# Feature groups with the heads innermost, and the constants of Ln as immediates, in a two-layer linear-attention kernel

## The chip, the cores and the metric

The kernel runs on one core of a Trainium2 chip. A core has five engines that this text speaks of: TensorE (PE in the profile; the loading of its weights is PEld), VectorE (DVE), ScalarE (ACT), GpSimd (POOL) and SyncE (SP), which here issues DMAs. They share an on-chip memory of 128 partitions, SBUF. TensorE writes its results to a second memory, PSUM. The metric is the device time of one execution in microseconds (us), as the median of several runs. Beside it stands one profiled execution, with its own time.

## The reference

`x` has 2048 rows of 512 numbers in bf16. Two layers follow each other, each of an attention and an MLP, both behind a layer norm and added to `x`:

```python
x = x + A(layernorm(x))      # attention
x = x + B(layernorm(x))      # MLP; this pair twice, with the same weights

def A(x):
    q, k, v = x @ wqkv                        # 32 heads of 16 each
    pq, pk = q @ w_phi[h], k @ w_phi[h]       # per head, 16 x 16
    phi_q = concat(softmax(pq), softmax(-pq)) # 32 features
    phi_k = concat(softmax(pk), softmax(-pk))
    kv, z = phi_k^T v, sum of phi_k over the rows
    return (phi_q kv / (phi_q z + 1e-6)) @ wo

def B(x):                                     # F = 1376
    return (relu(x @ W_gate) * (x @ W_up)) @ W_down
```

The layer norm divides by `sqrt(variance + 1e-5)`.

## The kernel before, in words

The 2048 rows are 16 tiles `t` of 128 rows, one row to a partition. `X` holds them in SBUF for the whole run.

**The softmax.** A softmax doesn't change when the same number is taken from all 16 inputs, so the kernel subtracts the last of them: 15 differences remain (`DF`), and the 16th Exp is 1. The subtraction is folded into the weights (`wf`, line 422; `Wblk`, line 426, a block-diagonal matrix of `w_phi` made from `wf` and the mask `Mf`; `Wk2` and `Wq2`, lines 481 to 486). TensorE then gives, for one tile, 480 differences of keys (line 596) or queries (line 656). ScalarE raises them twice, with scale 1 and -1 (line 568, `raised`), into a tile `ek` of 8 groups of 128 elements. A group belongs to four heads: 4 x 15 features for the plus sign, 4 x 15 for the minus sign, and 8 numbers that stand for the 16th features.

**The sums.** VectorE sums each run of 15 features, 64 sums for a tile (line 606 for keys, `sk`; line 661 for queries, `sq`). ScalarE takes Ln(1 + sum) and Exp of its negative (lines 615 and 618 for keys, 666 and 668 for queries), which is the reciprocal. For keys that goes into the last 8 of a group, and all 120 features are multiplied by their scale (`halves`, line 554, in two instructions of four groups each, each on GpSimd or VectorE). For queries VectorE makes the ratio of the two signs (line 672), and only the plus half is multiplied by it (line 677, GpSimd or VectorE).

**The rest of the attention.** The keys' features meet `v` in the state (`kvz`, line 629), which is summed over all 16 tiles. Then it is multiplied by a mask `Mg` that keeps each head's own block (`R`, lines 641 and 646). The queries' features are transposed by DMA (`fq`, line 682) and multiplied by `R` (line 693). The quotient (lines 700 to 707), `wo` (line 716) and the addition to `x` with a row sum (line 720) follow. The layer norm ahead of the attention takes statistics on VectorE (lines 510 and 511), Ln(variance + 1e-5) and Exp(-0.5 ...) on ScalarE (lines 518 and 520).

**The MLP** is gate and up (line 793), relu and product (lines 797 to 812), down (line 833) and the addition to `x` (line 840), in blocks of 1, 2 or 4 tiles.

**The order.** Every instruction's place is written out by hand: `ORDER` is the order in which all steps are issued, `SLOTS` says which buffer each takes, and `PLACE` on which of two engines a step runs where it has a choice. So each engine works a fixed list, and waits by semaphores for what its next instruction needs. The costs and due times that stand with each step no longer decide anything. The keys of all 16 tiles of a layer must be done before its state is, and layer 0's keys, queries and first MLP blocks share the first 80 us.

The lines that the change starts from (before):

```python
def features(ek, lo=0, n=NG):
    return ek.t[:, lo:lo + n, 0:2 * GF].rearrange("p g (j f) -> p g j f", f=DF)
...
v = features(ek, lo, n)
e.tensor_tensor(out=v, in0=v, in1=ek.t[:, lo:lo + n, 2 * GF:P].unsqueeze(3).to_broadcast(
    [P, n, 2 * HG, DF]), op=Alu.mult)
```

with `NG` = 8 groups, `HG` = 4 heads in a group, `DF` = 15 features, `GF` = 60.

Of the kernel before, what the change touches and what calls it, by code (L numbers as in the profile page):

```python
# [8 lines left out]
P = 128  # L9
# [4 lines left out]
NB = D // P  # L14
# [110 lines left out]
DVE0 = (85, 170)  # L125
# [3 lines left out]
NOTHING = (0, 0)  # L129
# [151 lines left out]
def kernel(  # L281
    ctx: ExitStack, tc: tile.TileContext, A_x, A_wqkv, A_w_phi, A_wo, B_x, B_W_gate, B_W_up,
    B_W_down, out):
    nc = tc.nc
# [8 lines left out]
    def new(name, shape, dt=BF16):  # L293
        return sb.tile([P] + shape, dt, name=name)
# [14 lines left out]
    wf = new("wf", [NB, DH])  # L309
    wgu, wd = new("wgu", [2, NB, F]), new("wd", [NF, D])  # L310
    ident = new("ident", [P])
    Mf, Mg, Mh = new("Mf", [HB], F32), new("Mg", [HG], F32), new("Mh", [HG], F32)
    Wblk = new("Wblk", [NB, HB * DF])
    R = new("R", [NG, GE])
    xnTA = [new(f"xnTA{c}", [C, NB, P]) for c in range(C)]
    eps, unit = new("eps", [1], F32), new("unit", [1], F32)
    rowsum, ssq = new("rowsum", [2, T], F32), new("ssq", [2, T], F32)
    wasteA, wasteD = new("wasteA", [D]), new("wasteD", [D])
    st = {(l, s): (new(f"bst{s}{l}", [T, 6], F32), new(f"mv{s}{l}", [T, 2], F32),
# [25 lines left out]
    def op(eng, cost, due, emit, deps=(), takes=(), uses=(), name="", **kw):  # L345
        o = Op(eng, cost, due, emit, deps, takes, uses, name, **kw)
        ops.append(o)
        return o
# [71 lines left out]
    c_m = op("DVE", (230, 330), 10, masks, [c_id], name="masks")  # L420
# [2 lines left out]
                                in1=wf[:, :, DF:DH].to_broadcast([P, NB, DF]), op=Alu.subtract)  # L423

    def blocks(e):
        e.tensor_tensor(
            out=Wblk[:].rearrange("p b (j f) -> p b j f", f=DF),
            in0=wf[:, :, 0:DF].unsqueeze(2).to_broadcast([P, NB, HB, DF]),
            in1=Mf[:].unsqueeze(1).unsqueeze(3).to_broadcast([P, NB, HB, DF]), op=Alu.mult)

    c_cen = op("DVE", (200, 290), 20, against_last, [l_wf], name="wcen", port=True)
    c_blk = op("DVE", (640, 740), 20, lambda: blocks(nc.vector), [c_m, c_cen], name="Wblk", port=True,
               alt=("POOL", (1016, 1058), lambda: blocks(nc.gpsimd), 3))
    def state_masks():
        nc.vector.tensor_reduce(out=Mg[:], in_=ident[:, 0:2 * GF].rearrange("p (s h f) -> p h s f", s=2, f=DF),
                                axis=AX.XY, op=Alu.add)
        nc.vector.tensor_reduce(out=Mh[:], in_=ident[:, 2 * GF:P].rearrange("p (s h) -> p h s", s=2), axis=AX.X,
                                op=Alu.add)
        nc.vector.tensor_tensor(out=Mg[:], in0=Mg[:], in1=Mh[:], op=Alu.add)
    c_mg = op("DVE", (400, 490), 15000, state_masks, [c_m], name="Mg")  # L440
    wps = Buf(p_q)

    one = nc.const_aps.tensor(1.0, (P, 512), BF16)
# [69 lines left out]
    def norm_A(l, tiles, dues, afters, by_pe=False):  # L513

        _, mv, rs, ln = st[l, "A"]
        t0, n = tiles[0], len(tiles)
        seen = [stats(l, "A", t, due, after) for t, due, after in zip(tiles, dues, afters)]
        a = op("ACT", ACT1, dues[-1], lambda: nc.scalar.activation(
            out=ln[:, t0:t0 + n], in_=mv[:, t0:t0 + n, 1], func=AF.Ln, scale=1.0, bias=eps[:]), seen + [c_eps], name="ln")
        a = op("ACT", ACT0, dues[-1], lambda: nc.scalar.activation(  # L520
            out=rs[:, t0:t0 + n], in_=ln[:, t0:t0 + n], func=AF.Exp, scale=-0.5), [a], name="rstd")
        made, i = [], 0
        while i < n:
            k = 1 if by_pe or i + 1 == n else 2
            xn, scaled = Buf(p_xn), []
            for j in range(k):
                t = tiles[i + j]

                def on_pool(t=t, j=j, xn=xn):
                    nc.gpsimd.tensor_scalar(out=nm[:, t:t + 1], in0=mv[:, t, 0:1], scalar1=-1.0, scalar2=0.0,  # L530
                                            op0=Alu.mult, op1=Alu.add)
                    nc.gpsimd.tensor_scalar(out=xn.t[:, j], in0=x_of(t), scalar1=nm[:, t:t + 1],
                                            scalar2=rs[:, t:t + 1], op0=Alu.add, op1=Alu.mult)
                scaled.append(op("DVE", SCALE, dues[i + j], lambda t=t, j=j, xn=xn: nc.vector.tensor_scalar(
                    out=xn.t[:, j], in0=x_of(t), scalar1=mv[:, t, 0:1], scalar2=rs[:, t:t + 1],
                    op0=Alu.subtract, op1=Alu.mult), [a], [] if j else [xn], [xn] if j else [], name="xnA", port=2,
                    alt=("POOL", (930, 975), on_pool, 3) if l == 0 else None))
            c, r = tiles[i] // C, tiles[i] % C
            made += [turn(xn, lambda c=c, r=r, k=k: xnTA[c][:, r:r + k], k, dues[i], scaled, [], [], "xnTA",
                          by_pe)] * k  # L540
            i += k
        return made


    def features(ek, lo=0, n=NG):
        return ek.t[:, lo:lo + n, 0:2 * GF].rearrange("p g (j f) -> p g j f", f=DF)

    def halves(name, ek, engs, due, after, uses):
        parts = []
        n = NG // len(engs)  # L550

        def phi(e, lo):
            v = features(ek, lo, n)
            e.tensor_tensor(out=v, in0=v, in1=ek.t[:, lo:lo + n, 2 * GF:P].unsqueeze(3).to_broadcast(  # L554
                [P, n, 2 * HG, DF]), op=Alu.mult)
        for k, e in enumerate(engs):
            ways = {"DVE": ("DVE", dve(480), lambda k=k: phi(nc.vector, k * n), 1),
                    "POOL": ("POOL", (956, 998), lambda k=k: phi(nc.gpsimd, k * n), 3)}
            _, cost, f, _ = ways[e]
            parts.append(op(e, cost, due, f, after, [], uses, name=name,  # L560
                            port=ways[e][3], alt=ways["POOL" if e == "DVE" else "DVE"]))
        return parts

    def raised(ek, ps, s, side):
        assert side == "K" or ek.slot in ONES and ek.slot not in spoilt
        if side == "K":
            spoilt.add(ek.slot)
        nc.scalar.activation(out=ek.t[:, :, s * GF:(s + 1) * GF], in_=ps.t[:, 0:FW].rearrange(  # L568
            "p (g e) -> p g e", e=GF), func=AF.Exp, scale=1.0 - 2.0 * s)

    class Keys:
        def __init__(self, l, before):
# [8 lines left out]
        def begin(self, sk, row, t, due, due_v, due_z, xT, phi_eng, v_eng="ACT"):  # L581
            c, i = t // C, t % C
            kp, vp = Buf(p_a), Buf(p_b)
            ek, vx = Buf(p_ek), Buf(p_v)
# [10 lines left out]
            else:  # L595
# [8 lines left out]
            v = evac(v_eng, due_v, lambda: vx.t[:, :, 0:GQ], lambda: vp.t[:].rearrange("p (b e) -> p b e", e=GQ),  # L604
                     [v] + ones, [vx], [vp], "vext")
            a = op("DVE", SUM16, due, lambda: nc.vector.tensor_reduce(  # L606
                out=sk.t[:, row, :].rearrange("p (g j) -> p g j", g=NG), in_=features(ek), axis=AX.X, op=Alu.add),
                e, [] if row else [sk], [ek, sk] if row else [ek], name="sk")
            self.sk.append(a)
            self.ks.append(k)  # L610
# [2 lines left out]
        def finish(self, begun):  # L613
            (done, v, sk, ek, *rest), due = begun[0], begun[0][5]
            a = op("ACT", RLN[0], due, lambda: nc.scalar.activation(  # L615
                out=sk.t[:, 0, :], in_=sk.t[:, 0, :], func=AF.Ln, scale=1.0, bias=unit[:]), [done, c_eps], (), [sk],
                name="lnk")
            a = op("ACT", REXP[0], due, lambda: nc.scalar.activation(  # L618
                out=ek.t[:, :, 2 * GF:P], in_=sk.t[:, 0, :].rearrange("p (g j) -> p g j", g=NG), func=AF.Exp,
                scale=-1.0), [a], (), [sk, ek], name="rk")  # L620
            self.scale(a, v, ek, *rest)
# [31 lines left out]
    def query(l, t, due, xT, behind, key):  # L653
        c, i = t // C, t % C
        qp, ek, sq, fq = Buf(p_a), Buf(p_eq), Buf(p_sq), Buf(p_fq)
# [3 lines left out]
        e = [op("ACT", act(FW), due, lambda s=s: raised(ek, qp, s, "Q"), [q], (), [qp, ek], name="Eq")  # L659
             for s in range(2)]  # L660
        a = op("DVE", SUM16, due, lambda: nc.vector.tensor_reduce(  # L661
            out=sq.t[:].rearrange("p (g j) -> p g j", g=NG), in_=features(ek), axis=AX.X, op=Alu.add),
            e, [sq], [ek], name="sq", follow=behind)
        pos, neg = (lambda: sq.t[:].rearrange("p (g s h) -> p g s h", s=2, h=HG)[:, :, 0, :],
                    lambda: sq.t[:].rearrange("p (g s h) -> p g s h", s=2, h=HG)[:, :, 1, :])
        a = op("ACT", RLN[0], due, lambda: nc.scalar.activation(
            out=pos(), in_=pos(), func=AF.Ln, scale=1.0, bias=unit[:]), [a, c_eps], (), [sq], name="lnq")
        a = op("ACT", REXP[0], due, lambda: nc.scalar.activation(
            out=pos(), in_=pos(), func=AF.Exp, scale=-1.0), [a], (), [sq], name="rq")

# [2 lines left out]
                                   op1=Alu.mult)  # L673

        def scale(e):
            v = ek.t[:, :, 0:GF].rearrange("p g (h f) -> p g h f", f=DF)
            e.tensor_tensor(out=v, in0=v, in1=ek.t[:, :, 2 * GF:2 * GF + HG].unsqueeze(3).to_broadcast(  # L677
                [P, NG, HG, DF]), op=Alu.mult)
# [167 lines left out]
    p = PAR  # L846
# [3 lines left out]
    for t in range(T):  # L850
# [8 lines left out]
        sk = begun[0][2] if begun else Buf(p_sk)  # L859
# [92 lines left out]
```

## Time and profile before

| | |
|---|---|
| median of 3 runs | 371.65 us (371.59 to 1351.57) |
| profiled execution | 371.77 us |
| its span, first to last instruction | 370.0 us |
| PE busy | 361.4 us (98%) |
| DVE busy | 272.0 us (74%) |
| ACT busy | 203.4 us (55%) |
| POOL busy | 86.6 us (23%) |
| granted TensorE clock | 1.00 throughout |

One of the three runs took 1351.57 us; the other two agree within 0.06 us. A group's row in the profile reads: line, engine, operation, output and input tiles, shapes, count, then busy time in us and the mean of one in ns, then the idle time ahead of it and what ended that. A row of a table by stage reads: stretch of the span, its length, then busy time and number of instructions of each engine. Busy time of PE is modelled, since matrix multiplications are pipelined: 98% busy is not PE at its peak.

### The profile page before, as it was taken

To read this page: it belongs to the slowest core of one execution; us is meant where nothing else is said; L and a number is where in the kernel's file an instruction comes from. 1 tells how busy PE (TensorE), PEld (TensorE's weight loads), DVE (VectorE), ACT (ScalarE), POOL (GpSimd) and SP (SyncE) were. 2 spreads that over 40 slices of the span, in tenths; PEclk is the share of its full clock that TensorE was granted. 3 is DMA by queue.
4 is the path that set the end of the run, shared out by engine and by line. 5 is a ranking of instruction groups with operands and counts; after the bars stand their busy time and mean duration, and the time that the engine had idled before them with its cause. 6 is when DMAs were issued, how large, how long until landed. Compare 5 with 4: busy or idle time off the path is not lost.

```text
span 370.0 us, 7444 instructions
## 1 busy us (share of the span) xinstructions
PE 361.4 (98%) x2803; PEld 217.0 (59%) x2845; DVE 272.0 (74%) x604; ACT 203.4 (55%) x549; POOL 86.6 (23%) x111
## 2 busy tenths in 40 slices
PE   8999999999999999999999999999999999999996
PEld 5454557776555454555666655686755454467484
DVE  6999999988798966848979498898976373233253
ACT  5999999662544860587274455874434226403130
POOL 4589754510030116004213173120000000000000
PEclk9999999999999999999999999999999999999999
DMA  8997776796653501113411210498752102010213
GB/s 239 195 225 161 235 123 128 128 151 126 96 101 58 99 16 30 37 22 64 85 36 31 57 32 0 69 134 121 137 99 45 28 0 44 0 44 0 81 54 98
DMA packets 93925, 31.73 MB, mean 86 GB/s; under 512 B 85345, under 2 KB 92865, under 8 KB 93889
## 3 DMA queue, kind: packets, MB, share of 16 engines
q1 hardware_dynamic: 93088, 30.98, 42.4%
q8 instruction: 22, 0.36, 0.4%
q10 hardware_dynamic: 800, 0.28, 0.3%
q14 instruction: 15, 0.11, 0.1%
HBM read 8.44 MB, written 2.10 MB: 28 GB/s over the span
## 4 chain that ended last, share of the span: by engine, by line
PE 84%; ACT 9%; DVE 2%; issue 1%; DMA 1%; POOL 1%; SPq 0%; DVEq 0%; ACTq 0%
PE b L793 38%; PE b L833 20%; PE b L716 7%; ACT ek L568 4%; PE b L601 4%; PE b L596 4%; PE b L656 4%; PE b L769 3%; PE q L693 2%; PE q L629 1%; ACT vext L453 1%; DMA X<-in_A_x_dram 1%; DVE sq L661 1%; ACT sk L615 1%; PE b L500 1%
## 5 line engine op out<-in xcount | busy, mean ns | idle before, releaser
L793 PE MATMUL b<-xnTB,wgu 128*128 128x128 bf16 (+2 forms) x1200 | 152.5, 279 | 0.1
L793 PEld LDWEIGHTS <-wgu 128*128 128x128 bf16 x1200 | 97.4, 98 | 47.2 <-issue 0.3
L797 ACT ACTIVATE gu<-b 128x512 bf16<-128x512 f32 (+1 forms) x83 | 47.6, 581 | 89.9 <-PE b L793 83.0
L833 PE MATMUL b<-wd,hT 128*128 128x512 bf16 (+3 forms) x340 | 83.2, 372 | 1.3
L568 ACT ACTIVATE ek<-b 128x480 bf16<-128x480 f32 x128 | 69.9, 597 | 16.1 <-PE b L596 8.6
L554 POOL TENSOR_TENSOR ek<-ek 128x480 bf16<-128x480 bf16 x48 | 49.5, 1055 | 79.2 <-ACT ek L618 74.6
L833 PEld LDWEIGHTS <-hT 128*128 128x128 bf16 (+1 forms) x363 | 34.3, 98 | 34.0 <-DVE hT L810 0.3
L810 DVE TENSOR_TENSOR hT<-gu,b 128x512 bf16<-128x512 bf16 (+1 forms) x44 | 28.6, 657 | 30.3 <-ACT gu L797 13.7
L677 POOL TENSOR_TENSOR ek<-ek 128x480 bf16<-128x480 bf16 x26 | 26.4, 1023 | 73.7 <-DVE ek L672 55.9
L661 DVE TENSOR_REDUCE sq<-ek 128x64 f32<-128x960 bf16 x32 | 36.4, 1144 | 4.1 <-ACT ek L568 4.1
L606 DVE TENSOR_REDUCE sk<-ek 128x64 f32<-128x960 bf16 x32 | 36.0, 1138 | 2.5 <-ACT ek L568 2.5
L801 DVE TENSOR_TENSOR hT<-gu 128x512 bf16<-128x512 bf16 (+1 forms) x39 | 17.2, 442 | 22.6 <-ACT gu L812 22.4
L840 DVE SCALAR_TENSOR_TENSOR X<-b,rsB,X 128x512 bf16<-128x512 f32 (+2 forms) x33 | 23.7, 729 | 12.9 <-PE b L833 12.7
L716 PE MATMUL b<-wo,oT 128*128 128x512 bf16 x117 | 30.8, 379 | 1.1 <-ACT oT L453 0.4
L601 PE MATMUL b<-wv,xnTA 128*128 128x512 bf16 x120 | 30.9, 379 | 0.6 <-ACT vext L453 0.2
L656 PE MATMUL b<-Wq,xnTA 128*128 128x480 bf16 x128 | 30.5, 365 | 0.1
L596 PE MATMUL b<-Wk,xnTA 128*128 128x480 bf16 x124 | 29.5, 366 | 0.0
L720 DVE SCALAR_TENSOR_TENSOR X<-b,X 128x512 bf16<-128x512 f32 x32 | 21.7, 684 | 6.0 <-PE b L716 5.8
L812 ACT CAST gu<-b 128x512 bf16<-128x512 f32 (+1 forms) x39 | 21.9, 573 | 6.8 <-PE b L793 6.6
L510 DVE BATCH_NORM_STATS2 bstA<-X 128x6 f32<-128x512 bf16 x32 | 21.4, 683 | 2.0 <-DMA X<-in_A_x_dram 1.7
L707 DVE TENSOR_TENSOR o<-q,rd 128x512 bf16<-128x512 f32 x32 | 21.9, 686 | 1.3 <-ACT rd L704 1.0
L601 PEld LDWEIGHTS <-xnTA 128*128 128x128 bf16 x128 | 12.0, 98 | 12.7 <-issue 0.3
(84 smaller groups left out, 346.4 us busy)
## 6 DMA issues: line engine op xcount, KB each, us to landing
out_dram<-X SPq DMA_DIRECT2D x15, 128.0 KB, 1.9
X<-in_A_x_dram SPq DMA_DIRECT2D x6, 256.0 KB, 4.8
wgu<-in_B_W_gate_dram SPq DMA_DIRECT2D x4, 344.0 KB, 3.7
wgu<-in_B_W_up_dram SPq DMA_DIRECT2D x4, 344.0 KB, 4.9
wd<-in_B_W_down_dram SPq DMA_DIRECT2D x5, 256.0 KB, 3.7
hT<-in_A_wqkv_dram SPq DMA_DIRECT2D x3, 256.0 KB, 4.4
X<-in_A_x_dram SPq DMA_DIRECT2D x4, 128.0 KB, 3.4
wv<-in_A_wqkv_dram SPq DMA_DIRECT2D x2, 256.0 KB, 4.8
```

What stands on the lines that cost most here:

```text
L554: e.tensor_tensor(out=v, in0=v, in1=ek.t[:, lo:lo + n, 2 * GF:P].unsqueeze(3).to_broadcast([P, n, 2 * HG, DF]), op=Alu.mult)
L568: nc.scalar.activation(out=ek.t[:, :, s * GF:(s + 1) * GF], in_=ps.t[:, 0:FW].rearrange("p (g e) -> p g e", e=GF), func=AF.Exp, scale=1.0 ...
L596: k = op("PE", mm(4, FW), due, lambda: [nc.tensor.matmul(kp.t[:, 0:FW], lhsT=xnTA[c][:, i, b, :], rhs=Wk2[:, b, :], start=(b == 0), stop=( ...
L601: v = op("PE", mm(4, 512), due_v, lambda: [nc.tensor.matmul(vp.t[:], lhsT=xnTA[c][:, i, b, :], rhs=wv[:, b, :], start=(b == 0), stop=(b == ...
L606: a = op("DVE", SUM16, due, lambda: nc.vector.tensor_reduce(out=sk.t[:, row, :].rearrange("p (g j) -> p g j", g=NG), in_=features(ek), axi ...
L656: q = op("PE", mm(4, FW), due, lambda: [nc.tensor.matmul(qp.t[:, 0:FW], lhsT=xnTA[c][:, i, b, :], rhs=Wq2[:, b, :], start=(b == 0), stop=( ...
L661: a = op("DVE", SUM16, due, lambda: nc.vector.tensor_reduce(out=sq.t[:].rearrange("p (g j) -> p g j", g=NG), in_=features(ek), axis=AX.X, ...
L716: a = op("PE", mm(4, 512), due + 3, lambda j=j, yp=yp: [nc.tensor.matmul(yp.t[:], lhsT=oT.t[:, j, b, :], rhs=wo[:, b, :], start=(b == 0), ...
L793: nc.tensor.matmul(ps.t[:, q * W:(q + 1) * W].rearrange("p (i t) -> p i t", t=P), lhsT=wgu[:, s, b, g * P:(g + 1) * P], rhs=xT.t[:, 0:n, b ...
L797: nc.scalar.activation(out=gu.t[:, 0, 0:cols], in_=gp.t[:, 0:cols], func=AF.Relu)
L810: nc.vector.tensor_tensor(out=h.t[:, f0 * W:f0 * W + cols], in0=gu.t[:, 0, 0:cols], in1=up.t[:, 0:cols], op=Alu.mult)
L833: nc.tensor.matmul(yp.t[:, 0:c1 - c0], lhsT=h.t[:m, f * W + i * P:f * W + (i + 1) * P], rhs=wd[:m, f, c0:c1], start=(f == 0), stop=(f == N ...
```

## The change

The 60 features of a sign and the 60 of the other no longer lie one behind the other, with each head's 15 together. A group's 120 features now lie as 15 rows of 8: row `f` holds feature `f` of the four heads with the plus sign and then of the four heads with the minus sign. The last 8 elements stay as they were. So:

- `Wblk` is made with the four heads innermost, by two instructions in place of one, and TensorE's 480 differences come out in the order group, feature, head.
- `raised` writes runs of 4 elements, every 8, where it wrote runs of 60.
- The sums read every eighth element, where they read neighbours.
- The multiplications read, as scales, the same row of 8 (keys) or 4 (queries) again for each feature, where they read each scale 15 times in a row. The queries' half is now rows of 4 in every 8.
- The mask `Mg` comes from one sum over `ident`, where it took three instructions.
- The Ln of the kernel take 1e-5 and 1.0 as immediates, where they read them from the tiles `eps` and `unit`; the two memsets of these tiles go.

No instruction changes its engine or its place in the order. TensorE, SyncE and all DMAs have the same lists as before.

```diff
-    eps, unit = new("eps", [1], F32), new("unit", [1], F32)
...
-        nc.vector.memset(eps[:], EPS)
-        nc.vector.memset(unit[:], 1.0)
-    c_eps = op("DVE", DVE0, 0, constants, name="eps")
+    c_eps = op("DVE", NOTHING, 0, lambda: None, name="eps")
...
-        e.tensor_tensor(
-            out=Wblk[:].rearrange("p b (j f) -> p b j f", f=DF),
-            in0=wf[:, :, 0:DF].unsqueeze(2).to_broadcast([P, NB, HB, DF]),
-            in1=Mf[:].unsqueeze(1).unsqueeze(3).to_broadcast([P, NB, HB, DF]), op=Alu.mult)
+        for g in range(2):
+          e.tensor_tensor(
+            out=Wblk[:].rearrange("p b (g f h) -> p b g f h", f=DF, h=HG)[:, :, g],
+            in0=wf[:, :, 0:DF].unsqueeze(3).to_broadcast([P, NB, DF, HG]),
+            in1=Mf[:, g * HG:(g + 1) * HG].unsqueeze(1).unsqueeze(1).to_broadcast([P, NB, DF, HG]), op=Alu.mult)
...
-        nc.vector.tensor_reduce(out=Mg[:], in_=ident[:, 0:2 * GF].rearrange("p (s h f) -> p h s f", s=2, f=DF),
-                                axis=AX.XY, op=Alu.add)
-        nc.vector.tensor_reduce(out=Mh[:], in_=ident[:, 2 * GF:P].rearrange("p (s h) -> p h s", s=2), axis=AX.X,
-                                op=Alu.add)
-        nc.vector.tensor_tensor(out=Mg[:], in0=Mg[:], in1=Mh[:], op=Alu.add)
+        nc.vector.tensor_reduce(out=Mg[:], in_=ident[:].rearrange("p (e h) -> p h e", h=HG), axis=AX.X, op=Alu.add)
...
-            out=ln[:, t0:t0 + n], in_=mv[:, t0:t0 + n, 1], func=AF.Ln, scale=1.0, bias=eps[:]), seen + [c_eps], name="ln")
+            out=ln[:, t0:t0 + n], in_=mv[:, t0:t0 + n, 1], func=AF.Ln, scale=1.0, bias=EPS), seen + [c_eps], name="ln")
...
     def features(ek, lo=0, n=NG):
-        return ek.t[:, lo:lo + n, 0:2 * GF].rearrange("p g (j f) -> p g j f", f=DF)
+        return ek.t[:, lo:lo + n, 0:2 * GF].rearrange("p g (f j) -> p g f j", f=DF)
...
-            e.tensor_tensor(out=v, in0=v, in1=ek.t[:, lo:lo + n, 2 * GF:P].unsqueeze(3).to_broadcast(
-                [P, n, 2 * HG, DF]), op=Alu.mult)
+            e.tensor_tensor(out=v, in0=v, in1=ek.t[:, lo:lo + n, 2 * GF:P].unsqueeze(2).to_broadcast(
+                [P, n, DF, 2 * HG]), op=Alu.mult)
...
-        nc.scalar.activation(out=ek.t[:, :, s * GF:(s + 1) * GF], in_=ps.t[:, 0:FW].rearrange(
-            "p (g e) -> p g e", e=GF), func=AF.Exp, scale=1.0 - 2.0 * s)
+        nc.scalar.activation(out=features(ek)[:, :, :, s * HG:(s + 1) * HG], in_=ps.t[:, 0:FW].rearrange(
+            "p (g f h) -> p g f h", f=DF, h=HG), func=AF.Exp, scale=1.0 - 2.0 * s)
...
-                out=sk.t[:, row, :].rearrange("p (g j) -> p g j", g=NG), in_=features(ek), axis=AX.X, op=Alu.add),
+                out=sk.t[:, row, :].rearrange("p (g j) -> p g j", g=NG), in_=features(ek).rearrange("p g f j -> p g j f"), axis=AX.X, op=Alu.add),
...
-                out=sk.t[:, 0, :], in_=sk.t[:, 0, :], func=AF.Ln, scale=1.0, bias=unit[:]), [done, c_eps], (), [sk],
+                out=sk.t[:, 0, :], in_=sk.t[:, 0, :], func=AF.Ln, scale=1.0, bias=1.0), [done, c_eps], (), [sk],
...
-            v = ek.t[:, :, 0:GF].rearrange("p g (h f) -> p g h f", f=DF)
-            e.tensor_tensor(out=v, in0=v, in1=ek.t[:, :, 2 * GF:2 * GF + HG].unsqueeze(3).to_broadcast(
-                [P, NG, HG, DF]), op=Alu.mult)
+            v = features(ek)[:, :, :, 0:HG]
+            e.tensor_tensor(out=v, in0=v, in1=ek.t[:, :, 2 * GF:2 * GF + HG].unsqueeze(2).to_broadcast(
+                [P, NG, DF, HG]), op=Alu.mult)
```

The sum and the Ln of the queries change in the same way as those of the keys.

More of the change, by code (lines that the diff above doesn't have):

```diff
@@ L311 @@
     ident = new("ident", [P])
-    Mf, Mg, Mh = new("Mf", [HB], F32), new("Mg", [HG], F32), new("Mh", [HG], F32)
+    Mf, Mg = new("Mf", [HB], F32), new("Mg", [HG], F32)
     Wblk = new("Wblk", [NB, HB * DF])
@@ L405 @@
     c_id = op("POOL", (900, 900), 0, first_constants, name="ident")
-    def constants():
-        nc.vector.memset(eps[:], EPS)
-        nc.vector.memset(unit[:], 1.0)
-    c_eps = op("DVE", DVE0, 0, constants, name="eps")
+    c_eps = op("DVE", NOTHING, 0, lambda: None, name="eps")
     ones = [op("DVE", DVE0, i, (lambda v: lambda: nc.vector.memset(v[:, :, GQ:GV], 1.0))(v), name="ones")
@@ L434, in state_masks @@
     def state_masks():
-        nc.vector.tensor_reduce(out=Mg[:], in_=ident[:, 0:2 * GF].rearrange("p (s h f) -> p h s f", s=2, f=DF),
-                                axis=AX.XY, op=Alu.add)
-        nc.vector.tensor_reduce(out=Mh[:], in_=ident[:, 2 * GF:P].rearrange("p (s h) -> p h s", s=2), axis=AX.X,
-                                op=Alu.add)
-        nc.vector.tensor_tensor(out=Mg[:], in0=Mg[:], in1=Mh[:], op=Alu.add)
-    c_mg = op("DVE", (400, 490), 15000, state_masks, [c_m], name="Mg")
+        nc.vector.tensor_reduce(out=Mg[:], in_=ident[:].rearrange("p (e h) -> p h e", h=HG), axis=AX.X, op=Alu.add)
+    c_mg = op("DVE", (230, 330), 15000, state_masks, [c_m], name="Mg")
     wps = Buf(p_q)
@@ L661, in query @@
         a = op("DVE", SUM16, due, lambda: nc.vector.tensor_reduce(
-            out=sq.t[:].rearrange("p (g j) -> p g j", g=NG), in_=features(ek), axis=AX.X, op=Alu.add),
+            out=sq.t[:].rearrange("p (g j) -> p g j", g=NG), in_=features(ek).rearrange("p g f j -> p g j f"), axis=AX.X, op=Alu.add),
             e, [sq], [ek], name="sq", follow=behind)
@@ L666, in query @@
         a = op("ACT", RLN[0], due, lambda: nc.scalar.activation(
-            out=pos(), in_=pos(), func=AF.Ln, scale=1.0, bias=unit[:]), [a, c_eps], (), [sq], name="lnq")
+            out=pos(), in_=pos(), func=AF.Ln, scale=1.0, bias=1.0), [a, c_eps], (), [sq], name="lnq")
         a = op("ACT", REXP[0], due, lambda: nc.scalar.activation(
```

## The prediction

> **What bounds the kernel now.** First the page: VectorE's busy tenths in forty slices of the span, and the chain that ended last, by engine.
>
> ```profile
> DVE  6999999988798966848979498898976373233253
> ...
> PE 84%; ACT 9%; DVE 2%; issue 1%; DMA 1%; POOL 1%; SPq 0%; DVEq 0%; ACTq 0%
> ```
>
> TensorE holds 84% of the chain, so over the whole run a faster VectorE or ScalarE buys little. But VectorE's row is full at its left end, and the change touches VectorE (DVE), ScalarE (ACT) and GpSimd (POOL) alone. So next the busy time by stage (columns as the first row says), and the chain in order of time (start, length, what) inside the first stage.
>
> ```profile
> core 0: us, PE busy (x) PEld busy (x) DVE busy (x) ACT busy (x) POOL busy (x), PEclk, DMA share, GB/s
> 14.00:20.00 6.00, 6.00 (x39) 2.89 (x38) 5.94 (x14) 6.00 (x20) 3.62 (x6) 1.00 0.89 155
> 20.00:40.00 20.00, 19.40 (x146) 10.14 (x146) 19.77 (x28) 20.00 (x60) 17.78 (x20) 1.00 0.94 205
> 40.00:60.00 20.00, 18.68 (x177) 10.48 (x178) 19.61 (x32) 19.37 (x58) 12.36 (x13) 1.00 0.78 173
> 60.00:80.00 20.00, 19.65 (x269) 16.53 (x271) 19.09 (x47) 13.86 (x45) 6.98 (x8) 1.00 0.68 121
> 80.00:160.00 80.00, 79.58 (x488) 42.99 (x494) 61.10 (x150) 39.35 (x107) 12.13 (x12) 1.00 0.41 72
> 160.00:240.00 80.00, 79.41 (x623) 48.16 (x630) 63.72 (x114) 48.53 (x129) 23.17 (x23) 1.00 0.23 42
> 240.00:260.00 20.00, 19.74 (x243) 15.26 (x245) 18.85 (x45) 11.69 (x39) 2.98 (x3) 1.00 0.85 129
> ```
>
> ```profile
> 31.71 2.30 ACT ek L568 x5
> ...
> 48.11 1.14 DVE sq L661
> ```
>
> From 14 to 80 us DVE is idle for 0.06 us and then for 60 - 58.47 = 1.53 us (58.47 is the sum of three rows). ACT is as full up to 60 us. There the chain runs through the Exp of line 568 and the sums of line 661, not through PE. After 80 us PE has no gap to speak of (79.58 of 80), and DVE has 18.9 us to spare up to 160 us, 16.3 us up to 240 us, but only 1.15 us from 240 to 260 us. Each engine works its list in a fixed order, and the order of the instructions doesn't change. So work added to DVE between 14 and 80 us, and between 240 and 260 us, moves everything behind it, and PE can't win the time back later.
>
> **The change part by part.** It leaves PE, SP and every DMA as they are. What changes is the order of elements inside a group of keys or queries: what were 15 neighbouring features of one head now lie eight elements, 16 bytes, apart.
>
> *The sums (lines 606, 661).* This is the part that decides. Each reads the same 960 elements as before, but one every 16 bytes instead of a neighbour each time.
>
> ```profile
> L661 DVE TENSOR_REDUCE sq<-ek 128x64 f32<-128x960 bf16 x32 | 36.4, 1144 | 4.1 <-ACT ek L568 4.1
> L606 DVE TENSOR_REDUCE sk<-ek 128x64 f32<-128x960 bf16 x32 | 36.0, 1138 | 2.5 <-ACT ek L568 2.5
> ...
> L417 DVE TENSOR_REDUCE Mf<-ident 128x8 f32<-128x128 bf16 x1 | 0.3, 286 | 1.3 <-POOL ident masks.py:199 1.3
> ```
>
> ```profile
> L801 DVE TENSOR_TENSOR hT<-gu 128x512 bf16<-128x512 bf16 x37 | 16.6, 451 | 21.1 <-ACT gu L812 21.0
> L554 DVE TENSOR_TENSOR ek<-ek 128x480 bf16<-128x480 bf16 x16 | 12.5, 794 | 0.9 <-ACT ek L618 0.8
> L677 DVE TENSOR_TENSOR ek<-ek 128x480 bf16<-128x480 bf16 x6 | 3.9, 650 | 0.0
> ...
> L801 DVE TENSOR_TENSOR hT<-gu 128x256 bf16<-128x256 bf16 x2 | 0.6, 289 | 1.4 <-ACT gu L812 1.4
> ```
>
> Between 128 and 960 neighbouring elements a sum grows from 286 to 1138 ns: 1.024 ns an element and 155 ns fixed. No sum of any length in this trace reads with such a jump, so its price is bounded. Below: nothing, if the adder and not the read sets the 1.024 ns. Nothing excludes that, but a gain is excluded, since no element is saved. Above: the slowest stream of 16-bit operands from SBUF here, POOL's 1055 ns for 480 elements (quoted below), 2.20 ns each; the sum would take 155 + 960 x 2.20 = 2265 ns, 1.13 us more. Between these ends I go by the only rows that show what DVE loses when neighbours are no longer neighbours: line 801 multiplies rows without jumps at (451 - 289)/256 = 0.633 ns an element with 127 ns fixed, line 677, one of whose operands repeats single elements, at (650 - 127)/480 = 1.09 ns, 1.72 times as much. Taken as a price of layout, a sum takes 155 + 960 x 1.024 x 1.72 = 1846 ns, **0.70 us more**. [...]
>
> [...]
>
> *The multiplications on DVE (lines 554, 677).* The scales are now rows of eight or four neighbours, so line 801 is the pattern: 127 + 480 x 0.633 = 431 ns. That saves 0.22 us against 650, and 0.36 us against the mean of 794 of the keys, which a few longer ones raise. At worst they stay as they are, because rows of four are shorter than those of line 801.
>
> How many of both fall into each stage (sums of keys, sums of queries, the keys' and then the queries' multiplications on DVE; busy time and count):
>
> ```profile
> 14.00:20.00 6.00, 3.23 (x3) 1.00 0.89 155
> 20.00:80.00 60.00, 14.37 (x13) 1.00 0.80 166
> 160.00:240.00 80.00, 13.72 (x12) 1.00 0.23 42
> ```
>
> ```profile
> 20.00:80.00 60.00, 18.03 (x16) 1.00 0.80 166
> 160.00:240.00 80.00, 8.02 (x7) 1.00 0.23 42
> 240.00:260.00 20.00, 5.71 (x5) 1.00 0.85 129
> ```
>
> ```profile
> 20.00:80.00 60.00, 5.33 (x7) 1.00 0.80 166
> 160.00:240.00 80.00, 5.90 (x7) 1.00 0.23 42
> ```
>
> ```profile
> 240.00:260.00 20.00, 1.93 (x3) 1.00 0.85 129
> ```
>
> *The Ln with immediates.* The constants' two memsets and a handful of tiny DVE instructions go before the first x has landed, where DVE waits anyway: nothing. A Ln no longer fetches a bias.
>
> ```profile
> L666 ACT ACTIVATE sq<-sq,unit 128x32 f32<-128x32 f32 x32 | 10.6, 336 | 2.8 <-DVE sq L661 2.5
> L668 ACT ACTIVATE sq<-sq 128x32 f32<-128x32 f32 x32 | 7.6, 236 | 0.4
> L704 ACT ACTIVATE rd<-rd 128x32 f32<-128x32 f32 x14 | 3.3, 233 | 0.3
> ```
>
> On the same 32 elements the Ln with a bias takes 336 and the Exp without one 236 ns, so 0.10 us goes from each; 29 of them between 20 and 80 us are 2.9 us of ACT. While DVE is the later of the two this buys nothing: the next stop is the sum.
>
> *The Exp (line 568)* writes runs of four elements, 8 bytes, with gaps of 8. Lines 668 and 704 take 236 and 233 ns for 32 elements in runs with gaps and without, so I cost it at nothing, with a rival for the case that short runs count. [...]
>
> *POOL (lines 554, 677, 426).*
>
> ```profile
> L554 POOL TENSOR_TENSOR ek<-ek 128x480 bf16<-128x480 bf16 x48 | 49.5, 1055 | 79.2 <-ACT ek L618 74.6 <-DVE ek L554 2.3 <-DVE xn L534 2.3
> L677 POOL TENSOR_TENSOR ek<-ek 128x480 bf16<-128x480 bf16 x26 | 26.4, 1023 | 73.7 <-DVE ek L672 55.9 <-ACT gu L797 9.7 <-issue 7.4
> ...
> L426 POOL TENSOR_TENSOR Wblk<-wf,Mf 128x480 bf16<-128x480 bf16 x1 | 1.0, 1000 | 1.0 <-DVE mvA L511 1.0
> ```
>
> Three patterns (repeated single scales twice, repeated rows against a repeated mask) lie within 6%, so I leave POOL at its times. Wblk becomes two halves: one more instruction, some 0.1 to 0.2 us before POOL's next x tile at the start, inside its waits there.
>
> *The sum*, DVE's work against the stage, only the excess counting:
> - 14 to 20 us: 3 x 0.70 - 0.06 = **+2.0**.
> - 20 to 80 us: 29 sums give +20.3; seven multiplications save 5.33 - 7 x 0.43 = 2.3, one of queries 0.2: 58.47 + 20.3 - 2.5 - 60 = **+16.3**.
> - 80 to 240 us: 27 sums (the 19 counted after 160 us and 8 before, what is left of the 64) are 18.9 us, beside 18.9 + 16.3 us idle; after 160 us, 63.72 + 13.3 - 5.90 + 7 x 0.43 = 74.1 of 80: **0**. That cover is thin; were it gone, some 3 us.
> - 240 to 260 us: 18.85 + 5 x 0.70 - 0.6 (three multiplications) - 20 = **+1.7**.
>
> Together +20.0. The profiled execution took 371.77 us (its span is 370.0), 0.12 us above the median 371.65: **391.8 us**, 5.4% slower. Every 0.1 us on a sum is worth some 3.5 us here. At the upper bound (1.13 us) the four terms are 3.3, 28.8, 2 and 3.9: 410 us.
>
> **The rivals.**
>
> *The sums don't notice the jump* (the other side: not slower). The adder sets the 1.024 ns. [...] Then DVE loses 2.5 us and ACT 2.9 us between 20 and 80 us, both being full there, and PE has 2.3 us of idle in those rows; the stage ends about 2.5 us earlier and the total is 369 us (367 to 371). It decides below 0.15 us a sum: there 29 x 0.15 = 4.4 us meet 2.5 us saved and 1.53 us idle.
>
> [...]
>
> *POOL minds the new pattern.* Half as long again, 0.5 us, on the 17 multiplications between 20 and 40 us would be 8.5 us beside 2.2 us idle: +6.3, with the sums unharmed 378 us. Against it: the three rows within 6%.
>
> *ACT minds the short runs.* From 32 to 480 elements Exp grows from 236 to 597 ns, 0.81 ns an element:
>
> ```profile
> L568 ACT ACTIVATE ek<-b 128x480 bf16<-128x480 f32 x128 | 69.9, 597 | 16.1 <-PE b L596 8.6 <-PE b L656 6.1 <-issue 1.3
> ```
>
> Doubled, that is 0.39 us each, two to a sum: 58 in the stage, 53.23 - 2.9 + 22.6 = 73 of 60 us, and 2.3 us before it: 387 us alone.
>
> **How the numbers follow.** The sums slower by 0.4 to 1.0 us: 0.56, 380 to 404 us, forecast 392. Over 404 us: 0.14. Sums unharmed: 0.20. POOL: 0.05, ACT alone: 0.05. A measurement of this kernel tells about 2% (7.4 us) from no change. Slower by more: 0.56 + 0.14 + 0.05 = 0.75; within: 0.20 + 0.05, less 0.02 for a gain of over 2%: 0.23. The range from 368 to 412 us leaves out about a third of the unharmed case (0.07) and half of the costliest (0.07).
>
> **What would show it.** Lines 600 and 655 of the changed kernel (the sums) at about 1850 ns, DVE at 10 of 10 tenths until some 98 us, PE with gaps there that end on DVE, the multiplications on DVE near 430 ns, the Ln of 32 elements near 236 ns, Exp and POOL within 5% of now. Sums that stay at 1140 ns make it wrong; so does PE found to run through while DVE lags, which would mean that the tiles in stock carry the delay.

## The result, and the profile after

The changed kernel takes 404.87 us (median), the kernel before 371.62 us: 33.25 us more, a ratio of 1.0896 (95% interval 1.0871 to 1.0920). The profiled execution of the changed kernel took 404.79 us, with a span of 403.0 us.

The groups of the changed kernel that the change touches (columns as before: busy us, mean ns of one, idle before). Its lines are numbered some seven lower: 599 and 654 are the sums, 547 and 670 the multiplications, 561 the Exp, 659 the queries' Ln.

```profile
L561 ACT ACTIVATE ek<-b 128x480 bf16<-128x480 f32 x128 | 68.1, 574 | 13.3 <-PE b L589 7.4 <-PE b L649 4.6 <-issue 1.3
L654 DVE TENSOR_REDUCE sq<-ek 128x64 f32<-128x960 bf16 x32 | 60.4, 1894 | 3.2 <-ACT ek L561 3.2
L599 DVE TENSOR_REDUCE sk<-ek 128x64 f32<-128x960 bf16 x32 | 59.8, 1883 | 2.0 <-ACT ek L561 2.0
...
L547 POOL TENSOR_TENSOR ek<-ek 128x480 bf16<-128x480 bf16 x48 | 48.7, 1036 | 92.1 <-ACT ek L611 87.2 <-DVE vext L447 2.7 <-PE q L622 2.2
...
L670 POOL TENSOR_TENSOR ek<-ek 128x480 bf16<-128x480 bf16 x26 | 26.3, 1018 | 92.4 <-DVE ek L665 76.2 <-ACT gu L790 11.5 <-DMA fq<-ek 3.6
...
L547 DVE TENSOR_TENSOR ek<-ek 128x480 bf16<-128x480 bf16 x16 | 8.3, 530 | 0.6 <-ACT ek L611 0.6
...
L659 ACT ACTIVATE sq<-sq 128x32 f32<-128x32 f32 x32 | 7.4, 232 | 19.6 <-DVE sq L654 19.4
...
L670 DVE TENSOR_TENSOR ek<-ek 128x480 bf16<-128x480 bf16 x6 | 2.4, 403 | 0.0
```

One kind of row has grown: a sum takes 1883 to 1894 ns where it took 1138 to 1144, 0.75 us more, on the same 960 elements. Every other row shown is shorter than its row before. The Ln of the queries now waits for its sum for 19.4 us in total, where it waited for 2.5.

The stages of the changed kernel, from its table by windows:

```profile
core 0: us, PE busy (x) PEld busy (x) DVE busy (x) ACT busy (x) POOL busy (x), PEclk, DMA share, GB/s
14.00:20.00 6.00, 5.77 (x30) 2.52 (x29) 6.00 (x11) 5.20 (x17) 3.21 (x6) 1.00 0.68 153
20.00:40.00 20.00, 14.49 (x101) 7.29 (x102) 20.00 (x23) 14.18 (x42) 12.55 (x16) 1.00 0.62 137
40.00:60.00 20.00, 13.95 (x105) 7.15 (x106) 20.00 (x18) 13.10 (x42) 9.83 (x10) 1.00 0.41 140
60.00:80.00 20.00, 17.77 (x206) 11.88 (x208) 19.97 (x33) 16.22 (x47) 9.21 (x9) 0.92 0.68 116
80.00:100.00 20.00, 16.73 (x193) 12.74 (x194) 19.89 (x37) 10.53 (x38) 4.96 (x5) 1.00 0.58 115
100.00:180.00 80.00, 77.42 (x470) 41.41 (x478) 65.64 (x150) 35.95 (x101) 12.37 (x12) 1.00 0.36 71
180.00:260.00 80.00, 74.58 (x526) 43.00 (x533) 68.33 (x98) 39.52 (x109) 21.43 (x21) 1.00 0.16 35
260.00:280.00 20.00, 17.36 (x230) 13.20 (x231) 18.13 (x33) 13.70 (x40) 4.04 (x4) 1.00 0.47 85
```

DVE is busy for 85.86 of the 86 us from 14 to 100 us, while PE falls to 14 of 20, and ACT, full there before up to 60 us, now waits (14.18 and 13.10 of 20). After 100 us DVE is not full (65.6 and 68.3 of 80), and yet PE loses 2.6 and 5.4 us in those two rows.

TensorE does the same instructions in the same order in both kernels, so the delay can be read at each of them: the start of the same weight load in both traces, and the difference.

```
start before  start after  delay (us)
     20.0         20.5       +0.5
     40.2         48.6       +8.5
     60.1         75.1      +15.0
     80.1         98.6      +18.5
    140.0        161.9      +21.9
    200.2        225.7      +25.5
    240.0        269.6      +29.5
    260.1        291.9      +31.8
    366.6        398.6      +32.0
```

18.5 us of the loss is there after the first stage, 11.0 us come between 80 and 240 us of before, 2.3 us between 240 and 260 us, and 0.2 us in all the rest of TensorE's work, where no sums are left. The two spans differ by 33.0 us. The last 1.0 us of that comes behind the last matmul. It is no matter of the stepped sums, since it is there without them too (All but the stepped sums): the last of the 16 parts of the final output transfer lands at 402.05 us, 1.0 us after the part before it, while in the kernel before all 16 land within 0.15 us.

### The profile page after: what moved, and what is told of

Read it like the earlier page. It is cut to its first block, busy times and chain, and to the rows that moved or that the text cites. A ratio compares the mean times of both kernels' runs of the same rounds, so it can differ in the third digit from the quotient of the medians.

```text
span 403.0 us, 7442 instructions
## 1 busy us (share of the span) xinstructions
PE 368.4 (91%) x2803; PEld 217.7 (54%) x2845; DVE 313.2 (78%) x600; ACT 198.3 (49%) x549; POOL 85.7 (21%) x112
## 5 line engine op out<-in xcount | busy, mean ns | idle before, releaser
L561 ACT ACTIVATE ek<-b 128x480 bf16<-128x480 f32 x128 | 68.1, 574 | 13.3 <-PE b L589 7.4
L547 POOL TENSOR_TENSOR ek<-ek 128x480 bf16<-128x480 bf16 x48 | 48.7, 1036 | 92.1 <-ACT ek L611 87.2
L654 DVE TENSOR_REDUCE sq<-ek 128x64 f32<-128x960 bf16 x32 | 60.4, 1894 | 3.2 <-ACT ek L561 3.2
L599 DVE TENSOR_REDUCE sk<-ek 128x64 f32<-128x960 bf16 x32 | 59.8, 1883 | 2.0 <-ACT ek L561 2.0
L826 PEld LDWEIGHTS <-hT 128*128 128x128 bf16 (+1 forms) x363 | 34.2, 98 | 36.9 <-issue 2.4
L670 POOL TENSOR_TENSOR ek<-ek 128x480 bf16<-128x480 bf16 x26 | 26.3, 1018 | 92.4 <-DVE ek L665 76.2
L649 PE MATMUL b<-Wq,xnTA 128*128 128x480 bf16 x128 | 31.5, 375 | 6.2 <-DVE vext L447 2.2
L713 DVE SCALAR_TENSOR_TENSOR X<-b,X 128x512 bf16<-128x512 f32 x32 | 21.8, 685 | 5.7 <-PE b L709 5.6
```

What stands on the lines that cost most here:

```text
L561: nc.scalar.activation(out=features(ek)[:, :, :, s * HG:(s + 1) * HG], in_=ps.t[:, 0:FW].rearrange("p (g f h) -> p g f h", f=DF, h=HG), fu ...
L599: a = op("DVE", SUM16, due, lambda: nc.vector.tensor_reduce(out=sk.t[:, row, :].rearrange("p (g j) -> p g j", g=NG), in_=features(ek).rear ...
L649: q = op("PE", mm(4, FW), due, lambda: [nc.tensor.matmul(qp.t[:, 0:FW], lhsT=xnTA[c][:, i, b, :], rhs=Wq2[:, b, :], start=(b == 0), stop=( ...
L654: a = op("DVE", SUM16, due, lambda: nc.vector.tensor_reduce(out=sq.t[:].rearrange("p (g j) -> p g j", g=NG), in_=features(ek).rearrange("p ...
L826: nc.tensor.matmul(yp.t[:, 0:c1 - c0], lhsT=h.t[:m, f * W + i * P:f * W + (i + 1) * P], rhs=wd[:m, f, c0:c1], start=(f == 0), stop=(f == N ...
```

## The experiments

The theory (theory 1 below) says that the sums' step of 16 bytes is the whole loss, and that the two layers' losses add. Its rivals give part of it to other edits, to the longer way of each tile, or to a stock of finished tiles that the first stage uses up.

### The immediates alone

```diff
 # the kernel before
-    ... func=AF.Ln, scale=1.0, bias=eps[:])
+    ... func=AF.Ln, scale=1.0, bias=EPS)
-    ... func=AF.Ln, scale=1.0, bias=unit[:])
+    ... func=AF.Ln, scale=1.0, bias=1.0)
```

> The kernel before with only the immediates in its 84 Ln. Theory 1 (the sums' step of 16 bytes is the whole loss): Ln of 32 elements 336 -> 232 ns, some 3 us of ScalarE work less between 20 and 80 us, but VectorE is as full there and keeps its sums and multiplications, so 370 to 371.6 us. Theory 2 (the immediates shorten the path by themselves, since the chain of that stage runs through ScalarE): 368 to 369.5 us.

370.22 us, a ratio of 0.9956 (0.9940 to 0.9971): 1.4 us less. Ln of 32 elements takes 239 ns instead of 336, yet only about half of the 3 us that ScalarE was to save in the stage comes through. The Ln of the queries, and the window from 20 to 60 us of this kernel:

```profile
L665 ACT ACTIVATE sq<-sq 128x32 f32<-128x32 f32 x32 | 7.5, 239 | 2.7 <-DVE sq L660 2.6
```

```profile
20.00:60.00 40.00, 38.87 (x344) 21.85 (x348) 39.18 (x63) 38.62 (x118) 30.61 (x32) 1.00 0.80 185
```

PE 38.87, DVE 39.18 and ACT 38.62 of 40 us: three engines stand within 0.6 us of each other. That fits a small gain from easing one of them; no run tests this reading by itself.

### The stepped sums alone

```diff
 # the kernel before, both sums
-    in_=features(ek), axis=AX.X
+    in_=ek.t[:, :, 0:2 * GF].rearrange("p g (f j) -> p g j f", f=DF), axis=AX.X
```

> The kernel before in which only the sums are changed: they read every eighth element of a group's 120, as after; what they add up is then no softmax sum, so the output is not the reference's, all the rest is as before. Theory 1 (the step of 16 bytes is the whole loss): sums 1885 to 1895 ns, and a time of at least the changed kernel's 404.9 us, 405 to 411 us, since the multiplications and Ln stay slow. Theory 2 (the sums account for the 22 us of the forecast's own sum at 0.745 us each, and some 11 us come from another part): 392 to 396 us.

407.60 us, a ratio of 1.0956 (1.0931 to 1.0981): 36.0 us more than before, 2.7 us more than the whole change.

```profile
L661 DVE TENSOR_REDUCE sq<-ek 128x64 f32<-128x960 bf16 x32 | 60.2, 1890 | 3.3 <-ACT ek L568 3.3
L606 DVE TENSOR_REDUCE sk<-ek 128x64 f32<-128x960 bf16 x32 | 59.6, 1875 | 2.1 <-ACT ek L568 2.1
```

So this edit alone makes the whole loss, and a little more.

### All but the stepped sums

```diff
 # the changed kernel, both sums
-    in_=features(ek).rearrange("p g f j -> p g j f"), axis=AX.X
+    in_=ek.t[:, :, 0:2 * GF].rearrange("p g (j f) -> p g j f", f=DF), axis=AX.X
```

> The changed kernel in which only the sums are changed back: they read neighbours, 15 by 15, which in the new order is no softmax sum, so the output is not the reference's. Theory 1: sums 1140 ns, 366 to 370 us, under the kernel before by what the multiplications on VectorE (530 and 403 ns instead of 794 and 650) and the Ln save. Theory 2 (another part costs some 11 us): 378 to 383 us.

370.66 us, a ratio of 0.9970 (0.9957 to 0.9983), sums at 1138 and 1144 ns. So the rest of the change, taken together, costs nothing. The time lies 0.7 us above theory 1's range: what the 22 cheaper multiplications on VectorE bring can't be told from the immediates alone (370.22 us). The window from 20 to 60 us shows which engine is next:

```profile
20.00:60.00 40.00, 39.11 (x348) 22.07 (x352) 38.53 (x63) 38.76 (x119) 29.63 (x32) 1.00 0.81 185
```

DVE is busy 0.65 us less than with the immediates alone, and PE, at 39.11 of 40 us, is now the fullest. At 300 us of before, this kernel's weight loads start 2.4 us earlier than before, and 2.1 us earlier with the immediates alone. The profiled execution loses some of that at its end: here too the last part of the output lands 1.0 us after the one before it.

### The price of a step, by itself

Sums over the gate and up weights, added to the very end of the kernel before, three of each kind, one kind to a line: 15 elements with a step of 1 to 32 elements, or 960 elements in runs of neighbours every 16 bytes. `flat` is the weights in one row, `into` a free tile. This kernel was run once.

```diff
+        def rows(step):
+            q = 960 // (15 * step)
+            return dict(out=into[:, 0:q * step].rearrange("p (q s) -> p q s", q=q), axis=AX.X, op=Alu.add,
+                        in_=flat[:, 0:q * 15 * step].rearrange("p (q f s) -> p q s f", q=q, f=15))
+        def runs(run):
+            q = 64 // run
+            return dict(out=into[:, 0:q], axis=AX.XY, op=Alu.add,
+                        in_=flat[:, 0:q * 15 * 8].rearrange("p (q f s) -> p q f s", q=q, f=15)[:, :, :, 0:run])
...
+        red(**rows(1)), red(**rows(1)), red(**rows(1))
...
```

> The kernel before with sums of 900 to 960 elements of the gate and up weights added at its very end, three of each: 15 elements with a step of 1, 2, 3, 4, 5, 6, 8, 10, 12, 16 and 32 elements (2 to 64 bytes), and then 960 elements in runs of 1, 2 and 4 neighbours every 16 bytes. If 16 bytes is a point from which a step costs: 1.02 ns an element up to 6 elements, about 1.8 from 8 on, and runs of 2 near 1.02, since each 16 bytes then gives two. If the price grows with the number of 16-byte pieces touched: already 1.3 to 1.6 ns at 5 and 6 elements. If it depends on the step alone and not on 16 bytes: different prices at 8, 10, 12, 16 and 32.

Its groups on VectorE from 367 us on, costliest first. Lines 933 to 943 have steps of 1, 2, 3, 4, 5, 6, 8, 10, 12, 16 and 32 elements of 2 bytes; lines 944 to 946 have runs of 1, 2 and 4.

```profile
L942 DVE TENSOR_REDUCE sk<-wgu 128x64 f32<-128x960 bf16 x3 | 5.6, 1859 | 0.1
L939 DVE TENSOR_REDUCE sk<-wgu 128x64 f32<-128x960 bf16 x3 | 5.6, 1856 | 0.1
L944 DVE TENSOR_REDUCE sk<-wgu 128x64 f32<-128x960 bf16 x3 | 5.5, 1832 | 0.1
L943 DVE TENSOR_REDUCE sk<-wgu 128x64 f32<-128x960 bf16 x3 | 5.3, 1755 | 0.1
L941 DVE TENSOR_REDUCE sk<-wgu 128x60 f32<-128x900 bf16 x3 | 5.2, 1745 | 0.1
L940 DVE TENSOR_REDUCE sk<-wgu 128x60 f32<-128x900 bf16 x3 | 5.2, 1736 | 0.1
L938 DVE TENSOR_REDUCE sk<-wgu 128x60 f32<-128x900 bf16 x3 | 4.1, 1370 | 0.1
L937 DVE TENSOR_REDUCE sk<-wgu 128x60 f32<-128x900 bf16 x3 | 3.5, 1174 | 0.1
L934 DVE TENSOR_REDUCE sk<-wgu 128x64 f32<-128x960 bf16 x3 | 3.5, 1153 | 0.1
L936 DVE TENSOR_REDUCE sk<-wgu 128x64 f32<-128x960 bf16 x3 | 3.5, 1153 | 0.1
L945 DVE TENSOR_REDUCE sk<-wgu 128x32 f32<-128x960 bf16 x3 | 3.5, 1153 | 0.1
L946 DVE TENSOR_REDUCE sk<-wgu 128x16 f32<-128x960 bf16 x3 | 3.5, 1153 | 0.1
L933 DVE TENSOR_REDUCE sk<-wgu 128x64 f32<-128x960 bf16 x3 | 3.5, 1150 | 0.1
L935 DVE TENSOR_REDUCE sk<-wgu 128x63 f32<-128x945 bf16 x3 | 3.4, 1138 | 0.1
```

With the prediction's 155 ns fixed cost taken off, an element costs 1.04 ns at steps of 2 to 8 bytes, 1.13 at 10, 1.35 at 12, and 1.76, 1.77 and 1.78 at 20, 16 and 32 bytes; at 64 bytes 1.67. So in these sums it is neither the neighbour (a step of 8 bytes leaves it and costs nothing, 1153 ns against 1150) nor the length of the step from 16 to 32 bytes (1.76 to 1.78 ns). What fits in kind is how often two reads in a row fall into the same 16 bytes: runs of two every 16 bytes cost nothing (line 945, 1153 ns against 1150), steps of 10 and 12 bytes, where some 16-byte pieces are met once and some twice, cost a part (1.13 and 1.35 ns an element). The size of that part isn't explained. Counted from the addresses, 30% of the reads at a step of 10 bytes and 53% at 12 are alone in their 16 bytes. At 0.73 ns for each of them (1.77 less 1.04) an element would cost an estimated 1.26 and 1.43 ns; measured are 1.13 and 1.35. The first expectation put steps of 5 and 6 elements at no cost and missed that; the second put them at 1.3 to 1.6 and holds at 6 (1.35), not at 5 (1.13).

Line against line: 1153 ns with two reads in each 16 bytes (945), 1832 to 1859 ns with one (944, 939, 942).

### A step of 8 bytes

```diff
 # the changed kernel: a sign keeps its 60 elements, in it 15 rows of 4 heads
-        nc.scalar.activation(out=features(ek)[:, :, :, s * HG:(s + 1) * HG], in_=...("p (g f h) -> p g f h") ...
+        nc.scalar.activation(out=ek.t[:, :, s * GF:(s + 1) * GF], in_=...("p (g e) -> p g e") ...
-            in_=features(ek).rearrange("p g f j -> p g j f"), axis=AX.X
+            in_=ek.t[:, :, 0:2 * GF].rearrange("p g (s f h) -> p g s h f", s=2, f=DF), axis=AX.X
-            v = features(ek, lo, n)      # keys: four groups, both signs
+            s = lo // n                  # keys: eight groups, one sign
+            v = ek.t[:, :, s * GF:(s + 1) * GF].rearrange("p g (f h) -> p g f h", f=DF)
```

> A third order of elements: each sign keeps its 60 elements, inside it 15 rows of the four heads. Sums read every fourth element, 8 bytes apart; Exp writes runs of 60 as before; the multiplications of keys go by sign, rows of four. It computes the whole reference. If 16 bytes is the point from which a step costs (two elements still share 16 bytes): sums 1140 ns, 365 to 369 us. [...]

369.67 us, a ratio of 0.9944 (0.9929 to 0.9959) to the kernel before. The sums are back:

```profile
L655 DVE TENSOR_REDUCE sq<-ek 128x64 f32<-128x960 bf16 x32 | 36.4, 1144 | 4.0 <-ACT ek L562 3.9
L600 DVE TENSOR_REDUCE sk<-ek 128x64 f32<-128x960 bf16 x32 | 36.0, 1138 | 3.4 <-ACT ek L562 3.4
...
L548 DVE TENSOR_TENSOR ek<-ek 128x480 bf16<-128x480 bf16 x16 | 8.2, 520 | 0.9 <-ACT ek L612 0.7
```

Each sum reads every fourth element at the price of neighbours, and the multiplications keep what the change gave them. This version does all that the change set out to do, and is faster than both kernels: 35.2 us under the changed one, 2.0 us (0.6%) under the one before. It lies 0.7 us above the range that I gave; from 20 to 60 us PE is the fullest engine again (39.04 of 40 us).

### Each layer alone

```diff
 # the changed kernel
+    def summed(ek, l):
+        if l == 0:        # the other run: l == 1
+            return features(ek).rearrange("p g f j -> p g j f")
+        return ek.t[:, :, 0:2 * GF].rearrange("p g (j f) -> p g j f", f=DF)
```

> The changed kernel with sums that step 16 bytes in layer 0 alone; those of layer 1 read neighbours, which in the new order is no softmax sum. Theory 1 (the two layers' losses add, each where its sums stand): the stage up to 80 us of before costs 18.5 to 20 us over the 370.7 us of the kernel with all sums near, 389 to 391 us. Theory 2 (the first stage uses up a stock of finished tiles, and the loss after 80 us comes from that): 396 to 402 us, nearly all of the loss.

> The same with the step in layer 1 alone. Theory 1: the rest of the loss, 14 to 16 us over 370.7, that is 384 to 387 us, although VectorE has 35 us idle between 80 and 240 us. Theory 2 (with the stock whole, the 27 sums in that stretch hide): 372 to 376 us, what the sums between 240 and 260 us cost.

Layer 0 alone: 392.90 us, 22.2 us over the kernel with near sums (370.66 us). Layer 1 alone: 383.23 us, 12.6 us. Together that is 34.8 us, and the changed kernel lies 34.2 us over the same mark. The losses add, and no stock carried from the one stage to the next is needed to explain them. The traces say the same: against the kernel with near sums, the weight loads with layer 0 alone are 22.6 us late at 80 us and just as late at 300 us. With layer 1 alone they are 0.9 us late from 40 to 100 us, which is no matter of its sums (the first starts at 95 us), and 13.3 us at 260 us. Layer 0 cost 2 to 4 us more than I expected, layer 1 some 1 to 4 us less. The 18.5 us that I went by were counted against the kernel before, ahead of which the rest of the change is already some 2 us by then; against the kernel with near sums the changed kernel is 21.8 us late at 80 us.

So why does layer 1 cost 12.6 us, where VectorE has idle time? The longest of what PE waited for in that run, from 100 to 270 us (in total, times, longest):

```profile
PE b L791 <- DVE X L718: 2.8, 3, 1.4
PE b L493 <- DVE xn L527: 1.4, 2, 0.8
PE q L627 <- ACT vext L446: 0.7, 1, 0.7
PE b L654 <- DVE ek L552: 0.7, 1, 0.7
PE q L691 <- DVE o L705: 0.7, 1, 0.7
PE b L493 <- DVE o L705: 0.6, 1, 0.6
```

The six make up 6.9 of the 12.6 us. Five of them wait for VectorE, each for a microsecond or so, and none for a sum itself: they wait for additions to `x` (line 718), scaled tiles (527), a multiplication (552) and quotients (705), which share VectorE's list with the sums. And VectorE's idle time in the kernel before is not spread evenly. Stretches of 5 us of it:

```profile
125.00:130.00 5.00, 4.96 (x11) 1.00 0.40 79
180.00:185.00 5.00, 5.00 (x8) 1.00 0.55 105
185.00:190.00 5.00, 4.84 (x12) 1.00 0.01 3
240.00:245.00 5.00, 4.97 (x10) 1.00 0.98 115
245.00:250.00 5.00, 4.96 (x14) 1.00 0.82 157
```

In these almost nothing more fits. Worked out over all 36 stretches of 5 us from 80 to 260 us (busy time plus 0.745 us for each sum that starts there, less 5, where that is above zero), the excess is 11.3 us. The same sum over stretches of 10 us gives 8.1, over 20 us 3.5, over the prediction's 80 us and 20 us 2.6. Measured: 12.6, and 14.9 between 80 and 260 us in the kernel before with stepped sums alone. The length of 5 us was chosen afterwards and follows from nothing: stretches of 2.5 us give 14.8, of 2 us 16.3. That full short stretches make the loss of layer 1 is thus argued from its size and from the waits, not tested by itself.

### The same time beside the sums

```diff
 # the kernel before, behind each of the 64 sums
+        nc.vector.tensor_reduce(out=extra[:], in_=ek.t[:, 0:6, 0:110], axis=AX.X, op=Alu.add)
```

> The kernel before, whole, with one more VectorE instruction behind each of the 64 sums, which adds up 660 neighbours into a tile that nobody reads: some 0.75 us of VectorE's time each, as much as the step of 16 bytes costs, but the Ln behind the sum needn't wait for it. Theory 1 (it is VectorE's time that is short, whoever uses it): as with the stepped sums in the kernel before, 404 to 409 us. Rival (a good part comes from the longer way through sum, Ln, Exp and multiplication of each tile): 390 to 400 us.

408.39 us, a ratio of 1.0991 (1.0974 to 1.1008): 36.8 us more than before, beside 36.0 us with the stepped sums in the same kernel.

```profile
L551 DVE TENSOR_REDUCE extra<-ek 128x6 f32<-128x660 bf16 x64 | 53.1, 829 | 0.0
```

The added instruction takes 829 ns, where the step adds 737 to 746 ns to a sum in that kernel: 12% more of VectorE's time, for 2% more loss. Against the kernel before, the weight loads are 22.2 us late at 80 us and another 13.5 us by 260 us; with the stepped sums it is 20.9 and 14.9. So VectorE's time, whoever uses it, is enough for nearly all of the loss, and the rival's 390 to 400 us are out. In layer 1, where more of VectorE's time cost 1.4 us less, a few us of the stepped sums' loss can still come from the longer way from Exp through sum and Ln to the product; these runs don't separate that.

## Why the prediction was right, and where it was off

The forecast was 391.8 us, 20.0 us for the change, in a range of 368 to 412 us. The direction and the main term were right; the time came out 13 us above the forecast.

- **The price of a sum**: forecast 0.70 us more, measured 0.75. The size was right, but the reason wasn't. The estimate carried over what the multiplications pay without neighbours (1.72 times); by it a step of 8 bytes would have cost the same, and it cost nothing (1138 and 1144 ns). The factors of the time for each element, 1.72 forecast and 1.76 measured ((1883 - 155)/(1138 - 155)), lie close by luck.
- **The stage from 14 to 80 us**: forecast +18.3, measured +18.5; of that, 2.0 were forecast up to 20 us and 0.5 measured. DVE was full until 98.6 us, as forecast, and its added work moved all that follows. The forecast's gaps on PE that end on DVE are there too, though 5.8 of PE's 15.6 us of waits from 14 to 100 us end on ACT, whose Ln wait for the sums (the queries' 19.4 us in all).
- **80 to 240 us**: this is the step that failed. It was costed at nothing, "beside 18.9 + 16.3 us idle", with 3 us if the cover were gone. It cost 11.0 us, of the 13 us by which 392 us falls short of 404.87. The idle time was counted over 80 us, as if any of it could take up the added work. The runs show otherwise: layer 1's sums alone cost 12.6 us, and PE's longest waits there end on what shares VectorE's fixed list with the sums. Counted over 5 us, the same trace of before gives 11.3 us for 80 to 260 us, the right size; which length to count over stays open.
- **240 to 260 us**: forecast +1.7, measured +2.3. Another 1.2 us come after 260 us, 1.0 of them behind the last matmul.
- **The multiplications on DVE**: forecast 431 ns, measured 403 for the queries and 530 as the mean for the keys. Their saving in time was too small to be told from no saving; PE is the fullest engine there once the sums are near.
- **The Ln**: forecast 0.10 us less each, measured 0.10 (336 to 232).
- **Exp and POOL**: costed at no change; 597 became 574, 1055 became 1036, 1023 became 1018 ns. Their rivals fall.
- **The rival that the sums don't notice the jump** falls as a statement about 16 bytes (0.75 us more a sum), and holds for 8 (1138 and 1144 ns). Its time, 369 us, was near what the version with steps of 8 bytes then took (369.67).
- **Over 404 us** (given 0.14): the time lies there by a microsecond. No run shows a sum dear enough for the upper part of that case (the 410 us of the upper bound go with 2.20 ns an element): in the changed kernel an element took 1.80 ns ((1883 - 155)/960). What carried the time past 404 us was the 11.0 us between 80 and 240 us, costed at nothing.

## What to carry to other kernels

Before an element order is changed for the sake of one instruction, look at what every other instruction reads of it: here 22 multiplications became faster by 0.25 us and 64 sums slower by 0.75 us, and half the step gave the one without the other (sums at 1138 and 1144 ns, the keys' multiplications at 520). When an engine with a fixed list gets more work, measure its idle time in short stretches, not over a stage: here 2 to 5 us gave 16 to 11 us, 20 us gave 3.5, and 12.6 was measured. And when several engines are full together, expect little from what one of them saves: here the immediates were to save some 3 us of ScalarE's work, with PE, DVE and ACT within 0.6 us of each other from 20 to 60 us, and the time fell by 1.4 us.

## What was unexpected in the hardware

- In the run of steps, a sum all of whose reads are alone in their 16 bytes paid about 0.73 ns more for each (1.77 less 1.04), with little difference from 16 to 32 bytes (1.76 to 1.78 ns an element); at 64 bytes an element cost a little less (1.67 ns). Where only some reads are alone, the extra cost, put down to them, was smaller: an estimated 0.3 and 0.6 ns for each at steps of 10 and 12 bytes ((1.13 - 1.04)/0.30 and (1.35 - 1.04)/0.53).
- The granted clock fell to 0.50 for 3.41 us behind one gap on PE, and not behind another. In the changed kernel, in three windows of 4 us:

```profile
56.00:60.00 4.00, 1.41 (x14) 0.75 (x14) 4.00 (x7) 1.81 (x8) 1.01 (x1) 0.98 0.00 0
60.00:64.00 4.00, 3.88 (x30) 2.15 (x31) 4.00 (x7) 4.00 (x12) 1.86 (x2) 0.59 0.97 73
64.00:68.00 4.00, 3.83 (x53) 2.35 (x50) 4.00 (x6) 2.76 (x11) 2.72 (x4) 1.00 0.88 204
```

PE was busy for 1.41 us of the first, and the granted clock of the second is 0.59. The trace has it at half speed for 3.41 us from 59.9 us on. But PE was busy for only 1.83 of the 4 us from 41 us on too, and the clock stayed at 1.00 up to 48 us. So these runs don't show what brings it down. The kernel before has no such stretch before its end; the one with stepped sums alone has four of 3.41 us. At half speed such a stretch can cost at most 1.7 us of PE's work (half of 3.41). VectorE stood idle for only 0.14 us from 14 to 100 us of the changed kernel, so the slower PE can't have held it up by more than that; layer 1 alone cost its 12.6 us with no such stretch before its end.
